# Q rows loaded in natural order from pair 13 on, filler products beside the first scatter, and two GpSimd loads moved behind it

## The chip, the cores and the metric

The kernel runs on one core of one Trainium2 chip. The metric is device time in microseconds (us), the median over runs: 372.13 us over 4 runs, from 369.82 to 373.18. The profile is of one further execution of 369.75 us, whose traced span is 368.1 us.

## The reference

Attention over batch 8, 8 heads, 576 tokens, head size 64, with a window of 32 tokens to each side and 8 global tokens, then a two-matrix block with a squared ReLU.

```python
scores = scale * np.matmul(q, k.transpose(0, 1, 3, 2))
mask = np.abs(pos[:, None] - pos[None, :]) <= window          # window = 32
mask = mask | is_global[:, None] | is_global[None, :]         # 8 global tokens
attn = softmax(np.where(mask, scores, -1e9)); x = np.matmul(attn, v)
h = x @ w_in; r = np.maximum(h, 0.0)                          # 4608x512 @ 512x2048
out = (s * (r * r) + b) @ w_out                               # 2048x512
```

## The kernel before

**Pairs.** Two heads of one batch are a pair; there are 32 (four to a batch), and the kernel walks through them in order. The 576 keys of a head are cut into five chunks of 120 plus the 8 global keys (128 in all). For a pair, `qk` (L479) does per chunk one matmul of K against the queries in its band, an exponential on ScalarE and a mask multiplication on VectorE; `pv` (L498) multiplies the result with V and with ones; `norm_steps` (L516) normalises on ScalarE and VectorE and writes the columns of `xt`, the transposed input of the second block. The global queries' rows are put into `xt` at positions read from the input by `scatter` (L552), eight small copies on GpSimd for a batch.

**The second block** is a generator, `moe_quanta` (L563). Each step is four matmuls of 128x128 by 128x512. `run_pair` (L649) puts about eight such steps between the eight slots of each pair, so that TensorE always has work. It can begin for a batch only after that batch's `scatter`. With the order of work written out by hand, each engine takes its instructions strictly in program order.

**Loads.** A DMA is issued by GpSimd (POOL's queue) or by SyncE (SP's queue). Pairs 0 to 7 are loaded "six rows to a partition": 96 partitions, each with six consecutive tokens of two heads (`load_kq`, L153, GpSimd, rounding to bf16 on the way). From pair 8 (`NSIX`) on, K comes in natural order (one token to a partition, five chunks of 120, `load_nat`, L161, two DMAs) in fp32, is rounded by `round_k` (L182) and transposed by a DMA, `turn_k` (L204). Q still comes six rows to a partition by one DMA (`load_q`, L188), is rounded on ScalarE by `round_q` (L199), and transposed on TensorE by `trans` (L422): six transposes of 96 columns (L430) and one of a zero tile of 4 columns (L436). `trans_b` (L462) copies the transposed Q out of PSUM in two VectorE copies (L469), one a head, and undoes the six-row order in the same copy: the inner step of what it reads is 96 elements. Loads are issued at the start of pair p for pair p + 5 (L886).

**The beginning.** Pairs 0 to 4 run in `first_pair` (L718), with no second block between them; single matmuls of a zero tile whose product nobody reads (`warm`, L712) are put in instead. In pair 1, slot 2, `globals_of`'s last two steps (`move`, L387) turn the global V rows of batch 0 on TensorE and leave their copies to SBUF (`gvx`, L394, ScalarE) on the list `later`, which is emptied in slot 3 behind that slot's exponential and the `rep` activation. `put_v` (L404) then writes them into `vring`, which `pv(0)` reads. GpSimd issues `load_kq(6)` and `load_v(6)` after pair 2, `load_w_out(1)` after pair 3, then does `scatter(0)` (L839), then issues `load_w_out(2)`, `load_kq(7)`, `load_v(7)`, `load_w_out(3)` (L849 to L852) and, at pair 4, `gather(1)` (L892): two indirect DMAs that fetch the global K and Q rows of the next batches into `gf`. Pair 5, slot 7, rounds `gf` to `gb` on VectorE (L366) and pair 6, slot 1, transposes `gb` on TensorE (`turn`, L373).

Of the kernel before, what the change touches and what calls it, by code (L numbers as in the profile page):

```python
# [16 lines left out]
P = 128  # L17
B, H, S, D = 8, 8, 576, 64
NG = 8
# [8 lines left out]
NCH = 5  # L28
KC = 120
HB = 60  # L30
# [5 lines left out]
NR = 5  # L36
NV = 4
NJ = 6
NP6 = S // NJ
NSIX = 8  # L40
KT0 = 16
NX = 3
N6 = NCH * KC // NJ
# [10 lines left out]
def view(ap, *dims):  # L54

    return bass.AP(
        tensor=ap.tensor, offset=ap.offset, ap=[list(ap.ap[0])] + [list(d) for d in dims]
    )
# [8 lines left out]
def kernel(  # L67
# [12 lines left out]
    nc = tc.nc  # L80
# [30 lines left out]
    six = {t: const.tile([P, NR, 2, NJ, D], BF16, name=f"six{t}", tag=f"six{t}") for t in "kq"}  # L111


    natk = const.tile([P, NV, NCH, 2, D], FP32)
    natb = const.tile([P, NV, NCH * P], BF16)

    natq = const.tile([P, NV, 2, NJ, D], FP32)

    xt = const.tile([P, 4, NX * S + 2 * HB * NCH - S], BF16)
    natv = const.tile([P, NV, NCH, 2, D], FP32)  # L120
# [5 lines left out]
    for t, eng in (("k", nc.sync), ("q", nc.scalar)):  # L126
        eng.dma_start(
            out=six0[t].rearrange("p (h x) -> p h x", h=2),
            in_=src[t][0, 0:2].rearrange("h (p j) d -> p h (j d)", j=NJ),
# [5 lines left out]
        out=gidx_p[:],  # L135
        in_=bass.AP(
            tensor=global_idx.tensor, offset=global_idx.offset, ap=[[0, P // NG], [1, NG], [1, 1]]
        ),
# [3 lines left out]
    qbufs = [const.tile([P, 2, LQ], BF16, name=f"qbd{i}", tag=f"qbd{i}") for i in range(3)]  # L142
# [17 lines left out]

    def load_nat(eng, t, p):  # L161
        bi, hp = divmod(p, 4)
        dst = natv if t == "v" else natk
        r = NG if t == "v" else 0
        for hh in range(2):
            o = src[t][bi, 2 * hp + hh, 0, 0].offset

            runs = [(0, NCH, KC)]
            if p == NPAIR - 1 and hh == 1:
                runs = [(0, NCH - 1, KC), (NCH - 1, 1, S - KC * (NCH - 1))]  # L170
            for c, nch, n in runs:
                eng.dma_start(
                    out=dst[r : r + n, p % NV, c : c + nch, hh],
                    in_=bass.AP(
                        tensor=src[t].tensor, offset=o + c * KC * D,
                        ap=[[D, n], [KC * D, nch], [1, D]],
                    ),
                )
# [7 lines left out]
        )  # L186

    def load_q(p):  # L188
        bi, hp = divmod(p, 4)
        nc.sync.dma_start(  # L190
            out=natq[:NP6, p % NV].rearrange("p h j d -> p h (j d)"),
            in_=q[bi, 2 * hp : 2 * hp + 2].rearrange("h (p j) d -> p h (j d)", j=NJ),
        )

    def qrow(p):
        flat = six["q"][:NP6, p % NR].rearrange("p h j d -> p (h j d)")
        return flat.rearrange("p (j h d) -> p j h d", j=NJ, h=2)

    def round_q(p):  # L199
        nc.scalar.copy(  # L200
            out=qrow(p).rearrange("p j h d -> p h j d"), in_=natq[:NP6, p % NV]
        )

    def turn_k(p):  # L204
        kts[p] = kqp.tile([P, KT0 + NCH * P], BF16, tag="kt", name="kt")
        nc.sync.dma_start_transpose(
            out=kts[p][:, KT0:].rearrange("p (c x) -> p c x", x=P), in_=natb[:, p % NV]
        )

    def load_v(eng, p):  # L210
        load_nat(eng, "v", p)
# [13 lines left out]
    dummy = const.tile([P, DM], BF16)  # L225
# [11 lines left out]
    for t in gqd:  # L237
# [18 lines left out]
    ident = const.tile([P, P], BF16)  # L256
# [4 lines left out]
        out=part[:], in0=rowi[:], scalar1=3, scalar2=7,  # L261
# [5 lines left out]
        out=half[:], in0=partf[:], scalar=2.0 * S, in1=half[:], op0=OP.mult, op1=OP.add  # L267
    )
    nc.vector.tensor_copy(
        out=six["k"][:NP6, 0].rearrange("p h j d -> p (h j d)"), in_=six0["k"]  # L270
# [48 lines left out]
    for t in gadd:  # L319
# [7 lines left out]
        out=band[:], in0=band[:], scalar1=(float(WIN) + 0.5) ** 2, scalar2=None, op0=OP.is_le  # L327
# [14 lines left out]
    def load_w_out(j):  # L342
        nc.gpsimd.dma_start(
            out=wout_t[:, 4 * j : 4 * j + 4], in_=w_out2[:, 4 * j : 4 * j + 4]
        )
# [7 lines left out]
    def flush():  # L353
        ops, later[:] = list(later), []
        for f in ops:
            f()
# [65 lines left out]
    def trans(t, p):  # L422
        if p < 6:
            ps = ps_m.tile([P, LQ], BF16, tag="moe", name="pst")
        else:
            ps = ps_s.tile([P, LQ], BF16, tag="s", name="pst")
        for j in range(NJ):
            n = N6 if j == NJ - 1 else NP6
            if t == "q" and p >= NSIX:
                nc.tensor.transpose(  # L430
                    ps[:, NP6 * j : NP6 * j + NP6],
                    qrow(p)[:, j].rearrange("p h d -> p (h d)"), ident[:NP6, :NP6],
                )
                if n > NP6:
                    x = n - NP6
                    nc.tensor.transpose(  # L436
                        ps[:, NP6 * NJ : NP6 * NJ + x], dummy[:x, 0:P], ident[:x, :x]
                    )
                continue
            for hh in range(2):  # L440
                nc.tensor.transpose(  # L441
                    ps[D * hh : D * hh + D, NP6 * j : NP6 * j + n],
                    six[t][:n, p % NR, hh, j], ident[:n, :n],
                )
        return ps
# [16 lines left out]
    def trans_b(p, later=later):  # L462
        ps = trans("q", p)

        def evac():
            n = HB // NJ
            for hh, eng in ((1, nc.scalar.copy if p < 6 else V), (0, V)):
                r = slice(D * hh, D * hh + D)
                eng(  # L469
                    out=view(qbufs[p % 3][r, hh], [P, NCH], [HB + NG, 2], [NJ, n], [1, NJ]),  # L470
                    in_=view(ps[r], [2 * n, NCH], [n, 2], [1, n], [NP6, NJ]),
                )
            if p >= NSIX:
                ktile[p] = kts[p][:, KT0 - NG : KT0 - NG + LQ]
                put_kq(p)

        later.append(evac)
# [74 lines left out]
    def scatter(bi):  # L552

        for i in range(NG):
            nc.gpsimd.tensor_copy(  # L555
                out=xt[:, :, S * (bi % NX) : S * (bi % NX) + S][:, :, ds(greg_p[i], 1)],
                in_=xgs[bi][:, :, i : i + 1],
            )
# [90 lines left out]
    def run_pair(p, nq, extra):  # L649
# [4 lines left out]
        for s in range(8) if p > 4 else range(NCH, 8):  # L654
            prev, later[:] = list(later), []
            now = []
            if s < NCH:
# [3 lines left out]
                if s == 4 and hp == 0 and bi > 1:  # L661
                    later.append(lambda: scatter(bi - 1))
                if s == 2 and NSIX <= p + 2 < NPAIR:
                    cast_v(G, p + 2)
            elif s == 5:
                if p + 1 < NSIX:
                    cast_v(A, p + 1)
                if 4 < p < NPAIR - 1:
                    trans_b(p + 1, now)
            elif s == 6 and 4 < p < NSIX - 1:  # L670
                trans_a(p + 1, now)
            for f in now + prev:
                f()
            if s == 0:
                pv(p - 1)
                pending.extend(norm_steps(p - 1))
            if s == 7 and p + 1 < NSIX:
                put_v(V, p + 1)
# [33 lines left out]
    def warm(n, ps=None):  # L712

        ps = ps or idle_bank()
        for _ in range(n):
            nc.tensor.matmul(ps[:], dummy[:, 0:P], dummy[:])  # L716

    def first_pair(p, extra={}):  # L718
# [40 lines left out]
        out=sel6[:], in0=view(idx6[:], [1, NJ], [0, NG]),  # L759
# [9 lines left out]
    for j in range(2):  # L769
        nc.gpsimd.dma_start(  # L770
            out=win_t[:, :, 1024 * j : 1024 * j + 1024],
            in_=w_in2[:, :, 1024 * j : 1024 * j + 1024],
# [10 lines left out]
        out=vkey[:], in0=kidx[:], scalar1=float(S) - 0.5, scalar2=None, op0=OP.is_le  # L783
    )
    for i in range(2):
        c = i * (NCH - 1)
        nc.vector.tensor_copy(
            out=gadd[i][:, GAP : GAP + NG], in_=view(vkey[:, c : c + 1], [0, NG])
# [3 lines left out]
        out=sel[:], in0=view(kidx[:], [1, NCH], [0, NG]),  # L792
# [8 lines left out]
    steps0 = globals_of(0)  # L801
# [16 lines left out]
    for p in (1, 2, 3, 4):  # L818
        first_pair(p, {
            0: [steps0[1], steps0[2]],  # L820
            2: steps0[3:],
            3: [lambda: put_v(V, 0)],
        } if p == 1 else {})
        if p == 1:
            for j in (1, 2, 3):
                put_v(None, j)
            load_v(nc.gpsimd, 5)
            load_w_out(0)
            greg_p = [
                nc.gpsimd.value_load(g32[:1, i, 0:1], min_val=0, max_val=S - 1)  # L830
                for i in range(NG)
            ]
        elif p == 2:
            load_kq(6)
            load_v(nc.gpsimd, 6)
        elif p == 3:
            load_w_out(1)
    flush()
    scatter(0)  # L839
    for i in (1, 2, 3):  # L840
        rows_of(i)
    gvall = const.tile([NG, (B - 2) * H * D], BF16)
# [2 lines left out]
    nc.sync.dma_start(  # L845
        out=view(natb[96:P], [DM, NV * NCH * P // DM], [1, DM]),
        in_=view(dummy[96:P], [0, NV * NCH * P // DM], [1, DM]),
    )
    load_w_out(2)  # L849
    load_kq(7)  # L850
# [25 lines left out]
    for p in range(4, NPAIR):  # L876
# [16 lines left out]
        if p == 5:  # L893
            for i in range(NG):
                nc.gpsimd.dma_start(
                    out=gvall[i : i + 1].rearrange("o (b h d) -> o b h d", b=B - 2, h=H),
                    in_=v[2:, :, ds(greg_p[i], 1), :].rearrange("b h o d -> o b h d"),
# [6 lines left out]
        if p >= 6 and p + 2 < NPAIR:  # L904
# [4 lines left out]
            for i, j in enumerate(todo):  # L909
                if j < NPAIR:  # L910
                    x = 4 if p in (8, 9) else 4 * i
# [66 lines left out]
```

## Time and profile before

| what | value |
|---|---|
| median of 4 runs | 372.13 us (369.82 to 373.18) |
| profiled execution, its span | 369.75 us, 368.1 us |
| TensorE busy | 349.8 us, 95% of the span |
| VectorE, ScalarE, GpSimd busy | 253.0, 229.9, 82.1 us |
| mean granted TensorE clock | 0.975 |
| Q copies out of PSUM on VectorE (L469) | 58 of 780 ns |
| Q transposes, six-row form, pairs 8 to 31 (L430, L436) | 144 and 24 |
| Q rounding on ScalarE (L200), K rounding (L183) | 24 of 842 ns, 24 of 733 ns |
| DMA share of its 16 engines, 42 to 57 us and 117 to 301 us | 1.21 and 0.57 |

How to read it: TensorE's busy time counts modelled ends of pipelined matmuls, so a busy TensorE is not one at its peak. A row of the timeline gives start, duration, engine, line, operation, output and inputs, the count of merged instructions, and in brackets the idle time ahead of it and what ended it. Rows "POOL ... DMA" are issues, not transfers. The DMA share adds up the time that packets took on 16 engines; since packets overlap on an engine it can pass 1.

### The profile page before, as it was taken

To read this page: it belongs to the slowest core of one execution; us is meant where nothing else is said; L and a number is where in the kernel's file an instruction comes from. 1 tells how busy PE (TensorE), PEld (TensorE's weight loads), DVE (VectorE), ACT (ScalarE), POOL (GpSimd) and SP (SyncE) were. 2 spreads that over 40 slices of the span, in tenths; PEclk is the share of its full clock that TensorE was granted. 3 is DMA by queue.
4 is the path that set the end of the run, shared out by engine and by line. 5 is a ranking of instruction groups with operands and counts; after the bars stand their busy time and mean duration, and the time that the engine had idled before them with its cause. 6 is when DMAs were issued, how large, how long until landed. Compare 5 with 4: busy or idle time off the path is not lost.

```text
span 368.1 us, 7826 instructions
## 1 busy us (share of the span) xinstructions
PE 349.8 (95%) x2824; PEld 184.2 (50%) x2824; DVE 253.0 (69%) x636; ACT 229.9 (62%) x439; POOL 82.1 (22%) x164
## 2 busy tenths in 40 slices
PE   6679799899999999999999999999999999999996
PEld 2344344455545445567655555455557644444444
DVE  6667677867777898878878887788787743423421
ACT  6669589657876677657766776677647742612610
POOL 6964852122032211133103100311020001000000
PEclk9669899999999999999999999999999999999999
DMA  5999999999877777756538973883332011002002
GB/s 123 187 186 215 197 215 195 177 189 251 138 183 175 171 165 177 176 119 122 123 108 232 198 165 108 231 188 82 104 117 68 2 59 57 0 30 86 0 32 85
DMA packets 101440, 50.00 MB, mean 136 GB/s; under 512 B 84224, under 2 KB 94368, under 8 KB 101400
## 3 DMA queue, kind: packets, MB, share of 16 engines
q1 hardware_dynamic: 92360, 37.03, 46.6%
q0 software_dynamic: 8544, 12.03, 16.1%
q8 instruction: 22, 0.36, 0.5%
q10 hardware_dynamic: 496, 0.43, 0.4%
q14 instruction: 18, 0.15, 0.2%
HBM read 41.97 MB, written 9.44 MB: 140 GB/s over the span
## 4 chain that ended last, share of the span: by engine, by line
PE 73%; DVE 8%; DMA 5%; ACT 4%; POOL 4%; issue 3%; SPq 1%; ACTq 0%; POOLq 0%
PE psh L578 29%; PE pso L597 25%; PE po L507 8%; PE pss L481 6%; DVE qbd L469 3%; DMA gf<-in_q_dram,grow 2%; PE pst L430 2%; DMA sixq<-in_q_dram 1%; POOL gf L289 1%; PE psw L716 1%; PE pst L441 1%; ACT ln L538 1%; DMA natq<-in_q_dram 1%; DVE em L488 1%; DMA natv<-in_v_dram 1%
## 5 line engine op out<-in xcount | busy, mean ns | idle before, releaser
L578 PE MATMUL psh<-xt,win_t 128*128 128x512 bf16 (+2 forms) x704 | 140.4, 344 | 2.6 <-POOL xt L555 2.6
L597 PE MATMUL pso<-wout_t,g 128*128 128x512 bf16 (+1 forms) x592 | 137.3, 374 | 0.0
L585 ACT ACTIVATE r<-psh 128x512 bf16<-128x512 f32 x144 | 88.5, 614 | 61.3 <-PE psh L578 55.5
L485 ACT ACTIVATE e<-pss 128x384 bf16<-128x384 f32 (+1 forms) x160 | 76.6, 482 | 50.9 <-PE pss L481 49.9
L578 PEld LDWEIGHTS <-win_t 128*128 128x128 bf16 x704 | 63.6, 98 | 57.8 <-issue 5.1
L588 DVE TENSOR_TENSOR g<-r 128x512 bf16<-128x512 bf16 x144 | 59.6, 428 | 39.9 <-ACT r L585 39.6
L597 PEld LDWEIGHTS <-g 128*128 128x128 bf16 x592 | 55.8, 98 | 59.3
L488 DVE TENSOR_TENSOR em<-e,mask 128x384 bf16<-128x384 bf16 (+1 forms) x160 | 61.8, 389 | 26.9 <-ACT e L485 26.9
L481 PE MATMUL pss<-qbd,kt 128*128 128x384 bf16 (+1 forms) x160 | 52.1, 328 | 5.3 <-DVE qbd L417 2.5
L469 DVE COPY qbd<-pst 64x600 bf16<-64x600 bf16 x58 | 45.2, 780 | 5.5 <-ACT qbd L469 4.3
L555 POOL COPY xt<-xg 128x4 bf16 x64 | 15.3, 239 | 95.9 <-DVE xt L544 92.3
L617 DVE SCALAR_TENSOR_TENSOR osb<-pso,s_bc,bias_row 128x512 f32<-128x512 f32 (+1 forms) x25 | 18.1, 725 | 26.9 <-PE pso L597 26.9
L214 POOL CAST vring<-natv 128x640 bf16<-128x640 f32 x27 | 22.2, 827 | 60.1 <-PE po L507 33.4
L481 PEld LDWEIGHTS <-kt 128*128 128x128 bf16 x160 | 15.7, 99 | 26.0 <-DVE qbd L417 7.0
L544 DVE TENSOR_TENSOR xt<-po,rep 128x600 bf16<-128x600 f32 x32 | 25.0, 780 | 2.4 <-ACT rep L541 1.1
L538 ACT ACTIVATE ln<-po 128x640 f32<-128x640 f32 x32 | 22.5, 703 | 5.7 <-PE po L507 5.4
L541 ACT ACTIVATE rep<-ln 128x640 f32<-128x640 f32 x32 | 24.1, 752 | 0.1
L507 PE MATMUL po<-em,vring 128*64 128x160 bf16 (+3 forms) x448 | 19.7, 224 | 2.3 <-DVE vring L406 1.9
L507 PEld LDWEIGHTS <-vring 128*64 128x64 bf16 x448 | 15.5, 110 | 11.4 <-issue 6.6
L200 ACT CAST sixq<-natq 96x768 bf16<-96x768 f32 x24 | 20.2, 842 | 0.0
L507 PE MATMUL po<-em,onesb 128*64 128x160 bf16 (+2 forms) x448 | 19.7, 226 | 0.2 <-DVE xt L544 0.2
L183 ACT CAST natb<-natk 120x640 bf16<-120x640 f32 x24 | 17.6, 733 | 0.0
(104 smaller groups left out, 211.7 us busy)
## 6 DMA issues: line engine op xcount, KB each, us to landing
natv<-in_v_dram SPq DMA_DIRECT2D x55, 150.0 KB
natk<-in_k_dram SPq DMA_DIRECT2D x47, 150.0 KB
natq<-in_q_dram SPq DMA_DIRECT2D x24, 288.0 KB
out_dram<-osb SPq DMA_DIRECT2D x23, 256.0 KB
wst<-in_moe_w_out_dram POOLq DMA_DIRECT2D x8, 512.0 KB, 5.3
out_dram<-osbh SPq DMA_DIRECT2D x9, 256.0 KB
win_t<-in_moe_w_in_dram POOLq DMA_DIRECT2D x2, 1024.0 KB, 16.0
wout_t<-in_moe_w_out_dram POOLq DMA_DIRECT2D x4, 512.0 KB, 10.5
```

The source lines that it names most:

```text
L469: eng(out=view(qbufs[p % 3][r, hh], [P, NCH], [HB + NG, 2], [NJ, n], [1, NJ]), in_=view(ps[r], [2 * n, NCH], [n, 2], [1, n], [NP6, NJ]),)
L481: nc.tensor.matmul(ps[:], ktile[p][:, P * c : P * c + P], qbufs[p % 3][:, :, LO[c] : HI[c]])
L485: nc.scalar.activation(e[:], ps[:], AF.Exp, scale=SCALE)
L488: later.append(lambda: nc.vector.tensor_mul(em[:], e[:], masks[c]))
L507: nc.tensor.matmul(po[D * hh : D * hh + D, a : a + n], onesb[:] if part else vring[:, p % NV, c, hh], emt[(p, c)][:, hh, x : x + n], start ...
L538: nc.scalar.activation(ln[:], po[:, LQ : 2 * LQ], AF.Ln)
L541: nc.scalar.activation(rep[:], ln[:], AF.Exp, scale=-1.0)
L544: lambda: nc.vector.tensor_tensor(out=view(xt[:, hp, x0:], [KC, NCH], [HB, 2], [1, HB]), in0=halves(po[:, 0:LQ]), in1=halves(rep[:]), op=O ...
L578: nc.tensor.matmul(psh[:, d0 : d0 + n], win_t[:, a, f * P : f * P + P], xt[:, a, x0 : x0 + n], start=(a == 0 and j == 0), stop=(a == 3), s ...
L585: nc.scalar.activation(r[:], psh[:], AF.Relu)
L588: later.append(lambda g=g, r=r: nc.vector.tensor_mul(g[:], r[:], r[:]))
L597: nc.tensor.matmul(pso[:, 0:nn], gl[f][:, u * P : u * P + P], wout_t[:, f, n0 : n0 + nn], start=(f == 0), stop=(f == 15),)
```

## The change

1. From pair 13 (`NSIXQ`) on, `load_q` loads Q in natural order, like K: two DMAs of 120 partitions by five chunks instead of one of 96 partitions (for the last pair one more, for the short chunk). `round_q` copies 120x640 elements straight, `trans` does five transposes of 128 columns over all 128 partitions, and `trans_b`'s two copies read PSUM with inner step 1.
2. For pairs 8 to 12 the sixth transpose takes 100 rows, and the transpose of the zero tile goes. Its rows 96 to 127 are zeroed once by a new DMA on SP.
3. In pair 1, slot 2, `later` is emptied at once (`flush`), so that the two `gvx` copies stand ahead of slot 3's exponential and `rep`.
4. Ahead of `scatter(0)`, 12 matmuls of the zero tile (`warm(12)`) are put on TensorE.
5. `load_w_out(1)` and `load_v(6)` are issued after `scatter(0)` instead of ahead of it.

```diff
+NSIXQ = 13
 def load_nat(eng, t, p):
-        dst = natv if t == "v" else natk
+        if t == "q":
+            dst = natq[:].rearrange("p n h j d -> p n (h j d)")[:, :, 0 : NCH * 2 * D]
+            dst = dst.rearrange("p n (c h d) -> p n c h d", c=NCH, h=2)
+        else:
+            dst = natv if t == "v" else natk
 def load_q(p):
+        if p >= NSIXQ:
+            load_nat(nc.sync, "q", p)
+            return
+    def qnat(p):
+        return six["q"][:, p % NR].rearrange("p h j d -> p (h j d)")[:, 0 : NCH * P]
 def round_q(p):
+        if p >= NSIXQ:
+            nc.scalar.copy(
+                out=qnat(p)[0:KC],
+                in_=natq[0:KC, p % NV].rearrange("p h j d -> p (h j d)")[:, 0 : NCH * P],
+            )
+            return
 def trans(t, p):
+        if p >= NSIXQ:
+            for c in range(NCH):
+                nc.tensor.transpose(
+                    ps[:, P * c : P * c + P], qnat(p)[:, P * c : P * c + P], ident[:]
+                )
+            return ps
             if t == "q" and p >= NSIX:
                 nc.tensor.transpose(
-                    ps[:, NP6 * j : NP6 * j + NP6],
-                    qrow(p)[:, j].rearrange("p h d -> p (h d)"), ident[:NP6, :NP6],
+                    ps[:, NP6 * j : NP6 * j + n],
+                    qrow(p)[:n, j].rearrange("p h d -> p (h d)"), ident[:n, :n],
                 )
-                if n > NP6:
-                    x = n - NP6
-                    nc.tensor.transpose(
-                        ps[:, NP6 * NJ : NP6 * NJ + x], dummy[:x, 0:P], ident[:x, :x]
-                    )
 def trans_b(p):
+                if p >= NSIXQ:
+                    eng(
+                        out=view(qbufs[p % 3][r, hh], [P, NCH], [HB + NG, 2], [1, HB]),
+                        in_=view(ps[r], [P, NCH], [HB, 2], [1, HB]),
+                    )
+                    continue
 for p in (1, 2, 3, 4):
-            2: steps0[3:],
+            2: [*steps0[3:], flush],
         elif p == 2:
             load_kq(6)
-            load_v(nc.gpsimd, 6)
-        elif p == 3:
-            load_w_out(1)
     flush()
+    warm(12)
     scatter(0)
+    load_w_out(1)
+    load_v(nc.gpsimd, 6)
...
+    nc.sync.dma_start(
+        out=view(six["q"][96:P], [384, 10], [1, 384]), in_=view(dummy[96:P], [0, 10], [1, 384])
+    )
     load_w_out(2)
```

More of the change, by code (lines that the diff above doesn't have):

```diff
@@ L195, in qrow @@
     def qrow(p):
-        flat = six["q"][:NP6, p % NR].rearrange("p h j d -> p (h j d)")
+        flat = six["q"][:, p % NR].rearrange("p h j d -> p (h j d)")
         return flat.rearrange("p (j h d) -> p j h d", j=NJ, h=2)
+    def qnat(p):
+        return six["q"][:, p % NR].rearrange("p h j d -> p (h j d)")[:, 0 : NCH * P]
     def round_q(p):
+        if p >= NSIXQ:
[4 more added lines that the diff above has]
+            return
         nc.scalar.copy(
-            out=qrow(p).rearrange("p j h d -> p h j d"), in_=natq[:NP6, p % NV]
+            out=qrow(p)[:NP6].rearrange("p j h d -> p h j d"), in_=natq[:NP6, p % NV]
         )
```

## The prediction

> **What bounds the kernel now.** I read the page's busy line first (TensorE 349.8 us of 368.1), then the chain that ended last, then the timeline of each stage that the change touches. From 66 us on TensorE is the bound: in the window 117 to 301 us it is busy 182.38 of 184 us, so there every TensorE nanosecond saved counts, and the only waits are short ones at pair boundaries, on VectorE's Q copies. Before 66 us it is loads and waits. The chain, in order of time, around the first scatter:
>
> ```profile
> 41.57 0.77 POOL wout_t L343
> 44.55 0.92 POOL natv L172
> 46.56 1.04 POOL gf L289
> 47.91 8.71 DMA gf<-in_q_dram,grow
> 57.52 0.73 ACT natb L183
> ```
>
> The start of pair 6 hangs on the gather of global rows, which GpSimd issues at 47.91 us and which lands 8.7 us later. The timelines (start, duration, engine, line, operation; in brackets the idle time before) of TensorE, then VectorE:
>
> ```profile
> 41.58 4.44 PE L578 MATMUL psh<-xt,win_t 128*128 128x512 bf16 x12 [2.64 <-POOL xt L555]
> 45.85 0.30 PE L481 MATMUL pss<-qbd,kt 128*128 128x320 bf16 x1
> ...
> 56.92 0.25 PE L373 MATMUL psg<-ident,gb 64*64 64x64 bf16 x4 [0.41 <-DVE gb L366]
> ...
> 65.92 0.31 PE L481 MATMUL pss<-qbd,kt 128*128 128x320 bf16 x1 [1.17 <-DVE qbd L417]
> ```
>
> ```profile
> 56.64 0.23 DVE L366 CAST gb<-gf 128x128 bf16<-128x128 f32 x1 [0.68 <-DMA gf<-in_q_dram,grow]
> ```
>
> So the 2.64 us wait for the scatter is real, but TensorE waits for `gf` 15 us later even so: a gain before 56.5 us is kept only if `gf` comes sooner. GpSimd's queue:
>
> ```profile
> 37.56 0.80 POOL L343 DMA_DIRECT2D wout_t<-in_moe_w_out_dram  x1
> 38.96 2.57 POOL L555 COPY xt<-xg 128x4 bf16 x8 [0.61 <-DVE xt L544]
> 41.57 0.77 POOL L343 DMA_DIRECT2D wout_t<-in_moe_w_out_dram  x1
> 42.33 0.68 POOL L156 DMA_DIRECT2D sixk<-in_k_dram  x1
> 42.99 0.65 POOL L156 DMA_DIRECT2D sixq<-in_q_dram  x1
> 43.63 1.84 POOL L172 DMA_DIRECT2D natv<-in_v_dram  x2
> 45.45 0.81 POOL L343 DMA_DIRECT2D wout_t<-in_moe_w_out_dram  x1
> 46.56 1.04 POOL L289 DMA_INDIRECT gf<-in_k_dram,grow  x1 [0.30 <-issue]
> 47.91 0.98 POOL L289 DMA_INDIRECT gf<-in_q_dram,grow  x1 [0.30 <-issue]
> ```
>
> The scatter is not held up by the two issues ahead of it: GpSimd is free at 38.36 and then waits 0.61 us for VectorE. And the DMA engines are full (share 1.21 from 42 to 57 us), landing GpSimd's loads in order of issue: by the DMA view, `load_kq(6)`'s Q lands at 34.71 + 7.6 = 42.3, `load_w_out(1)` at 37.56 + 8.2 = 45.8, `gf` at 56.6. The gather is late because of the bytes ahead of it.
>
> [...] after the 2.64 us idle the clock is 0.60 from 41.6 to 45.9, and after 1.90 us at 22 to 24 us it is 0.54 from 25.0 to 28.6. [...] L469 (step 96) takes 775 ns for 600 elements, while the step-1 copies of 64 elements (L377) take 184. [...]
>
> **The change, part by part.** All against the profiled 369.75 us (span 368.1 and 1.65 around it), 2.38 below the median; I carry differences over to the median.
>
> *Natural Q, TensorE.* Around 108.7 us the six transposes and the zero tile last from 108.70 to 109.16, 0.46 us. The starts of the six take about 0.26, so the zero tile costs 0.20. Five of 128 columns: [...] scaling the traced 43 ns for 96 columns gives 57. Pairs 13 to 31: 19 x (0.46 - 0.28) = -3.4. Pairs 8 to 12: 5 x 0.20 = -1.0. TensorE is full, so -4.4 counts in full; ends -2 [...] and -4.8.
>
> *Natural Q, VectorE.* [...] Two copies a pair, 19 pairs: -11.9 us of VectorE, which is not the bound. What it buys are boundary waits on L469 and L417: 0.36 at 121.6, 0.60 at 160, and 0.11, 0.09, 0.13, 0.13, 0.19, together -1.6. If the copies stay at 775: 0.
>
> *Natural Q, ScalarE, SP, DMA.* 19 x (842 - 733) = -2.1 us of ScalarE, hidden behind TensorE. SP issues one more DMA a pair, about 0.5 us on a queue that issues 4.4 us in a 9.4 us pair; queued behind are `load_v`, `turn_k` and `put_v`, needed two pairs later. A load becomes 1200 packets of 256 bytes instead of 192 of 1536: at 23 against 90 ns mean, 27.6 against 17.3 us over 16 engines, +0.6 us a pair, share +0.07 upon 0.57. Loads have some 20 us in hand. Cost 0; if the share reached 1 each pair would pay the 0.6.
>
> *Flush.* The gvx copies start at about 20.8 instead of 22.68, `put_v` at 21.5 instead of 23.27, `pv(0)` up to 1.8 us sooner; the exponential behind them starts 0.2 later. But `pv(1)` needs the `vring` DMA, issued at 23.32 and only 0.9 earlier at best (GpSimd's cast ends 22.4), and pair 5's Q lands at 21.07 + 15.9 = 36.97, 0.7 before its use at 37.66. I take -0.5 at 38.95 (0 to -0.7).
>
> *warm(12).* 12 x 0.216 = 2.6 us fills the 2.64 wait, at no cost. It keeps the clock: the 12 products behind take 2.6 instead of 4.27, -1.7. TensorE is ready for `turn` at 56.51 - 0.5 - 1.7 = 54.3.
>
> *The two issues, and the SP fill.* `load_w_out(1)` and `load_v(6)` go behind the scatter, with `load_w_out(2)`, `load_kq(7)`, `load_v(7)`, `load_w_out(3)` and the gather queued after them: 0.80 + 1.83 us of issue, less 0.5. More important, GpSimd's DMA queue runs dry when `load_kq(6)` lands at 42.3, while the next load, issued at 41.0, moves its first bytes about 2 us later (a `gf` on idle engines lands 2.5 us after its issue). Lost: a gap of 0.8, the head start that the two loads had (0.3), the 240 KB fill of rows 96 to 127 (1.2 us at 200 GB/s, 0.8 of it in the gap, so 0.4), and SP's loads of pair 8 starting 2.2 us sooner with a third of the engines (0.7): +2.2, so `gf` lands near 58.8. Bounds: 0 (the queue stays full) and +4.5 (SP takes half). `turn` then starts at 59.1: TensorE idles 4.8 us instead of 0.41. So the -2.2 gained is all spent and +2.2 is added. [...] +1.6 (0 to 1.8). The 1.17 us wait at 65.92, where VectorE is behind, shrinks by about 0.6. Sum of the beginning: +2.2 + 1.6 - 0.6 = +3.2.
>
> *Total.* -4.4 - 1.6 + 3.2 = -2.8: 366.95 in the profile, 369.3 as a median.
>
> **The rivals.** *The gather is not late* (0.34): the queue's backlog hides the later issue, `gf` lands at 56.6 as before. For it: the shares stay over 1 up to 57 us, and `gf` is bounded by bytes, not by its issue. Against: 0.8 MB of those bytes lie behind the scatter now. TensorE then idles 2.6 us before `turn`, half a chance of 1.6 us of slow clock: -6.0 + 0.8 = -5.2, 366.9.
> *The gather is much later* (0.13), the one on the slower side: the re-queued loads fall behind SP's loads of pairs 8 to 10, so each goes at half rate. In the 4 us from 52.7 to 56.6 the last `load_w_out` needed 3.3 us beside SP, against 2.1 alone; with six loads at that pace `gf` lands near 64. It decides from +6 us in all, a landing at 61.4 with the clock's cost. At 64: +7.4 + 1.6 - 0.6 - 6.0 = +2.4, 374.5.
> *The copies don't speed up* (0.06): [...] -2.8 + 1.6 = -1.2, 370.9.
>
> **How the numbers follow.** The likeliest (0.47) is the sum, 369.3, its own range 367.3 to 371.3. The range to hold 8 in 10 goes from 365.3 (the gather on time and a little of the clock's cost saved) to 373.8 (a gather some 4 us later than that). A measurement of this kernel can tell about 1% (3.7 us) from no change. Faster by over 1% (under 368.4): 0.30 from the first rival, 0.11 from the main case's lower end, 0.41. Slower by over 1% (over 375.9): the far end of the second, 0.09. Within: 0.50.
>
> **What would show it.** L469 in natural form near 460 ns and about 12 us less VectorE work; five transposes in 0.28 us; no zero-tile transposes; the 12 `psh` products at about 41 us in 2.6 us; `gf`'s Q landing near 59, a wait of 4 to 5 us at L373 and a clock well under 1 after it. Wrong would be: a `gf` landing by 57 (then the first rival), data waits on natural Q after 100 us, or boundary waits that stay although the copies are shorter.

## The result, and the profile after

The changed kernel takes 369.65 us (median of 32 runs, 368.06 to 370.79) beside 370.94 us of the kernel before in the same comparison (median of 53 runs, 369.02 to 373.9): ratio 0.9958, 95% interval 0.9944 to 0.9971, so 1.1 to 2.1 us faster, 1.56 by the ratio. That is within 1%, on the side and in the range forecast; the forecast of -2.8 lies outside the interval. The two profiled executions do not show the gain: 369.69 us (span 368.0) against 369.75 (span 368.1). They are one execution each, so the stages are compared instead, each from the first `pss` product of one pair to that of a later one. The table has the experiments too, which are explained below; us:

| kernel | pairs 0 to 7 end at | 7 to 13 | 13 to 31 | 31 to the end | span |
|---|---|---|---|---|---|
| before | 65.92 | 55.70 | 170.66 | 75.82 | 368.10 |
| **after** | **73.06** | **54.66** | **164.80** | **75.52** | **368.04** |
| e1, the issues put back | 68.86 | 55.28 | 164.80 | 75.51 | 364.45 |
| e3, natural Q only | 67.61 | 55.23 | 164.80 | 75.51 | 363.15 |
| e4, the move only | 73.51 | 56.30 | 170.69 | 75.82 | 376.32 |
| e5, `warm` only | 68.52 | 55.70 | 170.64 | 75.83 | 370.69 |
| e6, no zero tile, six-row Q | 67.60 | 55.86 | 168.59 | 75.75 | 367.80 |
| e9, flush only | 66.41 | 56.29 | 170.68 | 75.82 | 369.20 |

The column "13 to 31" answers one question exactly: it is 170.64 to 170.69 with six-row Q and its zero tile, and 164.80 with natural Q, in every kernel of the table. In the changed kernel the stages from pair 7 to the end, called the middle below, give 7.2 us (1.04 + 5.86 + 0.30), and the beginning takes 7.1 of it away in this execution. The first two columns are less steady. With the old Q, "7 to 13" lies between 55.70 and 56.30. Two of the experiments, e7 and e11, have the code of the changed kernel up to pair 13; their pairs 0 to 7 end at 73.69 and 71.66 us, where this profile has 73.06.

VectorE's Q copies, in the page's costliest groups (count, then busy us and mean ns, then the idle time before them), first before, then after in both forms:

```profile
L469 DVE COPY qbd<-pst 64x600 bf16<-64x600 bf16 x58 | 45.2, 780 | 5.5 <-ACT qbd L469 4.3
```

```profile
L494 DVE COPY qbd<-pst 64x600 bf16<-64x600 bf16 x20 | 15.6, 778 | 4.8 <-ACT qbd L494 4.5
L489 DVE COPY qbd<-pst 64x600 bf16<-64x600 bf16 x38 | 17.8, 468 | 0.9
```

The same 600 elements take 778 ns in the six-row form and 468 in the natural one; the forecast said near 460. That figure was an estimate of mine which the profile of before did not show. VectorE's busy time falls from 253.0 to 240.2 us.

TensorE's timeline around the first scatter, and on to the turn of pair 6:

```profile
40.08 2.76 PE L741 MATMUL psw<-dummy 128*128 128x512 bf16 x12
42.78 2.75 PE L603 MATMUL psh<-xt,win_t 128*128 128x512 bf16 x12
45.37 0.30 PE L506 MATMUL pss<-qbd,kt 128*128 128x320 bf16 x1
...
63.12 0.32 PE L391 MATMUL psg<-ident,gb 64*64 64x64 bf16 x4 [7.06 <-DVE gb L384]
63.37 1.89 PE L603 MATMUL psh<-xt,win_t 128*128 128x512 bf16 x4
```

Before, the line behind the turn reads:

```profile
57.10 1.04 PE L578 MATMUL psh<-xt,win_t 128*128 128x512 bf16 x4
```

The unread products fill the wait for the scatter, and the 12 `psh` products behind them take 2.59 us from first start to the next product (45.37 - 42.78) where they took 4.27. Then the gain is handed over: the wait at the turn, 0.41 us before, is 7.06, and four products after it take 1.89 us instead of 1.04, on half the clock (0.50 from 63 to 67 us). The chain that ended last goes through the same place:

```profile
50.40 1.01 POOL gf L307
51.72 11.10 DMA gf<-in_q_dram,grow
```

The gather is issued at 51.72 instead of 47.91 us and lands 11.1 us later instead of 8.7. GpSimd's timeline says what came ahead of it:

```profile
34.45 0.64 POOL L158 DMA_DIRECT2D sixq<-in_q_dram  x1
40.17 2.56 POOL L580 COPY xt<-xg 128x4 bf16 x8 [5.08 <-DVE xt L569]
42.77 0.76 POOL L361 DMA_DIRECT2D wout_t<-in_moe_w_out_dram  x1
43.52 1.83 POOL L178 DMA_DIRECT2D natv<-in_v_dram  x2
```

GpSimd sits idle for 5.08 us ahead of the scatter, and between 34.45 and 42.77 us it issues no load. What that does to the DMA engines stands in the windows (busy us and instructions of TensorE, its weight loads, VectorE, ScalarE, GpSimd; then clock, DMA share, GB/s), first before, then after:

```profile
40.00:44.50 4.50, 2.92 (x9) 1.12 (x9) 2.62 (x12) 1.25 (x4) 4.22 (x9) 0.76 1.15 191
```

```profile
40.00:44.50 4.50, 4.50 (x28) 1.98 (x23) 3.03 (x13) 2.40 (x5) 3.87 (x11) 1.00 0.34 67
63.00:67.00 4.00, 3.88 (x13) 1.49 (x14) 2.34 (x11) 1.60 (x3) 1.90 (x4) 0.50 1.11 216
```

In 40 to 44.5 us TensorE goes from 2.92 busy at a clock of 0.76 to full, which is what the `warm` line is for, and the DMA engines go from 191 to 67 GB/s. (191 - 67) x 4.5 us = 0.56 MB were not moved in that stretch: 2.8 us of transfer at 200 GB/s, the rate of before from 42 to 57 us. The line from 63 us on has the slow clock that follows the wait, 0.50.

### The profile page after: what moved, and what is told of

Read it like the earlier page. It is cut to its first block, busy times and chain, and to the rows that moved or that the text cites. A ratio compares the mean times of both kernels' runs of the same rounds, so it can differ in the third digit from the quotient of the medians.

```text
span 368.0 us, 7804 instructions
## 1 busy us (share of the span) xinstructions
PE 348.6 (95%) x2793; PEld 184.4 (50%) x2793; DVE 240.2 (65%) x636; ACT 227.9 (62%) x439; POOL 85.4 (23%) x164
## 4 chain that ended last, share of the span: by engine, by line
PE 78%; DVE 6%; DMA 5%; POOL 4%; issue 3%; ACT 2%; POOLq 0%; ACTq 0%
PE pso L622 31%; PE psh L603 30%; PE po L532 8%; PE pss L506 6%; DMA gf<-in_q_dram,grow 3%; DVE qbd L494 2%; PE pst L447 2%; PE pst L460 1%; DMA sixq<-in_q_dram 1%; POOL gf L307 1%; DMA natk<-in_k_dram 1%; POOL natv L178 1%; DVE em L513 1%; PE psw L741 1%; DVE kt L431 1%
## 5 line engine op out<-in xcount | busy, mean ns | idle before, releaser
L513 DVE TENSOR_TENSOR em<-e,mask 128x384 bf16<-128x384 bf16 (+1 forms) x160 | 59.4, 374 | 29.5 <-ACT e L510 29.4
L580 POOL COPY xt<-xg 128x4 bf16 x64 | 19.2, 299 | 99.2 <-DVE xt L569 95.8
L494 DVE COPY qbd<-pst 64x600 bf16<-64x600 bf16 x20 | 15.6, 778 | 4.8 <-ACT qbd L494 4.5
L489 DVE COPY qbd<-pst 64x600 bf16<-64x600 bf16 x38 | 17.8, 468 | 0.9
```

Of the source, the lines that this page charges most:

```text
L494: eng(out=view(qbufs[p % 3][r, hh], [P, NCH], [HB + NG, 2], [NJ, n], [1, NJ]), in_=view(ps[r], [2 * n, NCH], [n, 2], [1, n], [NP6, NJ]),)
L513: later.append(lambda: nc.vector.tensor_mul(em[:], e[:], masks[c]))
```

## The experiments

The theory when they began: the middle's gain is the form of Q; the beginning's loss is the move of the two issues, which empties GpSimd's DMA queue and makes `gf` late. The rivals: the loss comes from SP's side (its earlier loads and the 240 KB fill) or from the flush; the middle's gain is TensorE's alone.

**e1: the two issues back, everything else as changed.**

```
         load_kq(6)
+        load_v(nc.gpsimd, 6)
+    elif p == 3:
+        load_w_out(1)
...
     scatter(0)
-    load_w_out(1)
-    load_v(nc.gpsimd, 6)
```

> The changed kernel with load_v(6) and load_w_out(1) issued ahead of the scatter again. Theory (the two loads behind the scatter leave GpSimd's DMA queue dry for some 4 us and put 0.8 MB ahead of the gather): gf's Q lands by 58 instead of 62.8, the wait at the transposes of gb falls from 7.1 us to about 3, and the kernel is 5 to 7 us faster than before, near 364.5. Rival (the lateness comes from the fill of the spare Q rows on SP, or from the scatter itself being 1.2 us late after the flush): gf still lands at 61 or later and the time stays within 1.5 us of the changed kernel.

Measured: 366.03 us, ratio 0.9823 (0.9772 to 0.9874). So in the changed kernel the move costs about 5 us by the runs (3.6 between the two profiled spans). `gf` lands at 59.12 instead of 62.82, later than the 58 expected. TensorE at the turn:

```profile
59.43 0.25 PE L391 MATMUL psg<-ident,gb 64*64 64x64 bf16 x4 [3.57 <-DVE gb L384]
```

Half of the wait goes with the move. The scatter's copies start at 39.99 us, after GpSimd has waited 0.88 us for VectorE, and at 40.17 us with the issues behind it: the two issues ahead of the scatter had not held it up.

**e3: natural Q only**, on the kernel before (with the fill of rows 96 to 127 that it needs).

> The kernel before with the Q parts alone (natural rows from pair 13, no zero tile for pairs 8 to 12, the fill on SP); no flush, no filler products, issues where they were. Theory (the whole gain of the middle, 7.2 us from pair 7 to the end, comes from the form of Q): 6 to 7.5 us faster than before. Rival (part of those 7.2 us is the engines catching up after the long wait at pair 6, so that it is not there without that wait): 3 to 5 us faster.

Measured: 365.18 us, 0.9819 (0.9782 to 0.9856). That is 6.7 us by the ratio, as the theory had it (5.0 between the profiled spans), and the stages from pair 7 on give 6.6 (0.47 + 5.86 + 0.31). The changed kernel has 0.6 more there, all of it in pairs 7 to 13; the rival of catching up would explain that part, but no run shows that it does. The waits list of TensorE from 117 to 301 us has no wait for VectorE left; before has three there, 1.2 us in all. `gf` lands at 57.44, only 0.8 later than before, and TensorE does not wait for it, so the fill is cheap for the gather where the queue stays full. Pair 7 starts 1.7 us later than before all the same: ScalarE stands for 2.46 us ahead of an exponential at 49.71 us (2.38 us in e6, in no other kernel), and the profile names nothing that it waited for.

**e4: the move only**, the e1 diff reversed, on the kernel before.

> The kernel before with the two issues moved behind the scatter, nothing else. Theory: the queue runs dry from about 42 to 43.6, gf lands at 59 to 61, TensorE waits 3 to 4.5 us at the transposes of gb and the clock halves after it: 3 to 6 us slower than before. Rival (the move costs nothing by itself, the lateness needs the flush or the fill): within 1 us of before.

Measured: 376.48 us, 1.0112 (1.0073 to 1.0152). `gf` is issued at 52.27 and lands at 63.26, the turn waits 5.31 us, and the DMA rate in 40 to 44.5 us is 25 GB/s. With no other edit the move makes the kernel 4.2 us slower, within the 3 to 6 expected; the landing and the wait are both longer than expected.

**e5: `warm(12)` only**, on the kernel before.

```
     flush()
+    warm(12)
     scatter(0)
```

> The kernel before with the 12 filler products ahead of the scatter alone. Theory (the 1.7 us of clock that they save are spent at the wait for gf, which is bounded by the DMA queue): the 12 products behind the scatter take 2.7 us instead of 4.4, the wait at the transposes of gb grows from 0.4 to 2 us or more, and the time is within 1.5 us of before. Rival (the gain is kept): 1.7 us faster or more.

Measured: 372.23 us, 1.0031 (1.0008 to 1.0054). TensorE's timeline of it:

```profile
42.37 2.75 PE L578 MATMUL psh<-xt,win_t 128*128 128x512 bf16 x12
...
59.08 0.25 PE L373 MATMUL psg<-ident,gb 64*64 64x64 bf16 x4 [3.47 <-DVE gb L366]
```

The products are fast and the time gained is waited away at the turn, as the forecast said of a gain ahead of `gf`; here `gf` also landed 2.2 us later (58.78 against 56.62), which was not forecast, and the clock was half from 59.9 to 63.3 (the four products behind the turn took 1.28 us instead of 1.04). The edit by itself gains nothing and costs a little.

**e9: the flush only**, on the kernel before.

```
-            2: steps0[3:],
+            2: [*steps0[3:], flush],
```

> The kernel before with the flush in pair 1 alone. Theory (the flush loses, because VectorE's small copy of gkt into kt then meets GpSimd's DMA issue and its three casts and takes 2.5 us instead of 0.16): that copy takes over 2 us again, pair 2 starts about 1 us later than before, and the end is 0 to 1 us later, since the wait for gf takes up what the beginning gains or loses. Rival (the 2.5 us were chance in one execution): the copy takes about 0.16 us, pair 2 starts 1.5 us sooner, the end is within 0.5 us of before.

Measured: 372.57 us, 0.9999 (0.9984 to 1.0013): nothing. VectorE's and then GpSimd's timeline of it:

```profile
21.11 2.55 DVE L413 COPY kt<-gkt 128x40 bf16<-128x40 bf16 x1
```

```profile
21.57 2.06 POOL L214 CAST vring<-natv 128x640 bf16<-128x640 f32 x3
```

The same copy before:

```profile
20.99 0.17 DVE L413 COPY kt<-gkt 128x40 bf16<-128x40 bf16 x1
```

The `gvx` copies do start sooner, but `put_v(0)` stands on VectorE behind a copy of 40 elements a partition, which lasts 2.55 us and ends within 0.04 us of GpSimd's third cast. The same copy takes 2.55 us in the changed kernel, 2.57 in e1, 2.27 in e3 and 2.02 in e4. Of these profiles it takes 0.17 only in that of before, where it started in a pause of GpSimd's (0.57 us long). The copy's recorded start (21.11) is 0.46 us ahead of the first cast's, more than the 0.17 us that it takes in before, and it lasts until all three casts are done (21.57 + 2.06 = 23.63), not one. The reading is that the casts hold the copy; by what means is not shown.

**e13: those casts moved to ScalarE**, on the changed kernel, to test that reading.

```
-    for p in (1, 2, 3):
-        cast_v(G, p)
...
             for j in (1, 2, 3):
+                cast_v(A, j)
+            for j in (1, 2, 3):
                 put_v(None, j)
```

> The changed kernel with the casts of V for pairs 1 to 3 on ScalarE behind pair 1 instead of on GpSimd ahead of it. Theory (the flush gains nothing because VectorE's small copies, and put_v behind them, wait until GpSimd's casts are done): the copy of gkt ends 2 us sooner, pv(0) starts near 22.2 instead of 24.3, the scatter starts 0.5 to 1.5 us sooner and the end comes 0.5 to 2 us sooner than in the changed kernel. Rival (something else holds those copies): they still take over 2 us.

Measured: 371.25 us, 1.0003 (0.9986 to 1.0021), so about 0.4% slower than the changed kernel. VectorE, then TensorE:

```profile
21.34 0.22 DVE L431 COPY kt<-gkt 128x40 bf16<-128x40 bf16 x1
21.77 0.47 DVE L424 COPY vring<-gvx 8x640 bf16<-8x640 bf16 x1
```

```profile
22.29 1.01 PE L532 MATMUL po<-em,vring 128*64 128x160 bf16 x14
...
30.10 0.61 PE L532 MATMUL po<-em,vring 128*64 128x160 bf16 x14 [2.81 <-DMA vring<-gvx]
```

The hold is gone (0.22 us, though this copy too starts while GpSimd issues a load) and `pv(0)` starts at 22.29 instead of 24.35: the casts were the cause. The next pair's product then waits 2.81 us for the `vring` DMA, and the scatter starts at 41.42 us instead of 40.17, so the forecast of a gain at the end was wrong. Part of that wait is this edit's own: pair 1's cast now comes later, and SyncE issues the DMA at 24.17 us instead of 22.23. Whether the DMA would have held up the flush's gain by itself is not shown.

**e10: the gather first**, on the changed kernel: `gather(1)` ahead of the moved issues.

```
     scatter(0)
-    load_w_out(1)
-    load_v(nc.gpsimd, 6)
     for i in (1, 2, 3):
         rows_of(i)
+    gather(1)
+    load_w_out(1)
+    load_v(nc.gpsimd, 6)
...
-        if p % 8 == 4 and p + 4 < NPAIR:
+        if p % 8 == 4 and 4 < p and p + 4 < NPAIR:
```

> The changed kernel with one thing moved: the gather of the next batches' global rows is issued straight after the scatter, ahead of load_w_out(1), load_v(6) and the rest. Theory (the two moved loads cost time only because the gather is queued behind them): gf lands near 46 to 48, the wait of 7 us at the transposes of gb goes, the clock stays full, and the kernel is 6 to 8 us faster than the changed kernel, 362 to 364. Rival (a queue run dry costs more than the gather: the V and Q rows of pairs 6 and 7 come late as well): waits at the transposes of Q or at V's casts in pairs 5 to 7 take the gather's place, and the kernel stays within 3 us of the changed one.

Measured: 367.99 us, 0.9865 (0.9823 to 0.9907). `gf` lands at 48.05, and the turn still comes late. ScalarE, then TensorE:

```profile
57.08 0.72 ACT L232 CAST vring<-natv 128x640 bf16<-128x640 f32 x1 [5.12 <-DMA natv<-in_v_dram]
```

```profile
59.82 0.25 PE L391 MATMUL psg<-ident,gb 64*64 64x64 bf16 x4 [3.58 <-DVE gb L384]
```

ScalarE stands before the V of pair 6 instead, now behind the gather, with its next activations behind it. The bracket names `gb`, but `gf` had landed 11 us before: the cast of `gb`, at 59.56 us, stood on VectorE behind products that waited 3.70 us for ScalarE. Both forecasts missed: the wait moved, as the rival said, but the kernel is some 3.4 us faster than the changed one, neither 6 to 8 nor under 3. Of the some 5 us that the move costs, the new order thus saves 3.4; the bytes that the empty queue did not move are still missing, now to the V of pair 6.

**e8: natural Q and `warm`, no flush, issues back, gather first.**

> Natural Q and the 12 filler products, no flush, the two loads ahead of the scatter as in the kernel before, and the gather straight after the scatter. Theory: as e10, with no dry queue either; no wait for gf, the 1.7 us of clock kept: 8 to 10 us faster than before, 361 to 364. Rival (the saturated DMA engines deliver whatever is now queued behind the gather late instead): 6 to 7 us faster, no better than natural Q alone.

Measured: 364.81 us, 0.98 (0.9763 to 0.9837): the turn does not wait and the clock is full from 30.6 us on (the four products behind the turn take 1.04 us). That is 7.4 us faster than before, less than the 8 to 10 expected. It is about 1.6% below the changed kernel, the lowest ratio found, but not to be told from e1, e3 or e12. Much of what it saves in the beginning against e3 (pair 7 starts at 65.23 us, not 67.61) it gives back: pairs 7 to 13 take 56.82 us where e3 takes 55.23, in waits of 0.4 to 0.7 us for VectorE at the pair boundaries.

**e12: e8 with natural Q from pair 8** (`NSIXQ = 8`).

> The kernel of e8 (no flush, loads ahead of the scatter, gather straight after it, filler products) with natural Q from pair 8 on instead of 13. Theory (TensorE and the boundary waits bound the pairs from 8 on too): the waits of 0.3 to 0.7 us at 82 to 113 us go and the transposes shrink, 2 to 3.5 us faster than e8, near 361. Rival (the loads for pairs 8 to 12 are issued while the DMA engines are full, and natural rows take 27.6 us of engine time against 17.3): Q comes late, ScalarE waits for it, and it is no faster than e8 or slower.

Measured: 364.6 us, 0.9818 (0.9787 to 0.9848), no better than e8: TensorE waits 1.38 us at 63.9, ahead of pair 7, and pairs 7 to 13 take 58.05 us, with a wait of 2.20 at 82.6. VectorE's line there:

```profile
84.49 0.17 DVE L431 COPY kt<-gkt 128x40 bf16<-128x40 bf16 x1 [3.37 <-DMA kt<-natb]
```

The rival had the time right, but not the wait: it is for K, not for Q. SyncE issues this transposing of K by DMA at 80.59 us, where e8 has it at 77.22. In SyncE's order it stands behind the Q loads, which now need two issues each instead of one; what share of the delay they make is not shown.

**e6: six-row Q throughout, without the zero tile.** The rows 96 to 127 are filled, and the sixth transpose reads 100 rows. The edit is against e3's kernel.

```
-NSIXQ = 13
+NSIXQ = 99
```

> The kernel before with six-row Q to the end, but no zero tile for pairs 8 to 31 (the sixth transpose takes 100 rows, with the fill on SP). Theory (the zero tile costs 0.20 us of a full TensorE in each pair): 24 x 0.20 = 4.8 us faster, between 4 and 5.5. Rival (at pair boundaries TensorE waits for VectorE's Q copies, so that what is saved comes back as a longer wait there): 2 to 3.5 us faster.

Measured: 369.59 us, 0.9912 (0.988 to 0.9943), 3.3 us faster, as the rival had it. The stage from 13 to 31 is what it was made for. TensorE has 18 x 0.196 = 3.5 us less to do and the stage is 2.07 shorter. The waits of TensorE from 117 to 301 us (total, times, longest), before and then in e6:

```profile
PE pss L481 <- DVE qbd L417: 1.2, 3, 0.6
```

```profile
PE pss L506 <- DVE qbd L435: 3.2, 8, 0.8
```

So what TensorE saved came back as waits for VectorE. In pairs 7 to 13, where five zero tiles went, nothing was gained (55.86 against 55.70). Natural Q's transposes are no shorter than these (0.279 us against 0.262), yet with it the stage is another 3.79 shorter, and the 3.2 us of waits are gone. What differs is VectorE's Q copy, 0.31 us each of two, and ScalarE's rounding (752 ns in the changed kernel against 842).

**e7 and e11: the natural copy made longer,** to isolate it: in e7 it walks the elements in another order, in e11 it is a product with ones.

```
-                        out=view(qbufs[p % 3][r, hh], [P, NCH], [HB + NG, 2], [1, HB]),
-                        in_=view(ps[r], [P, NCH], [HB, 2], [1, HB]),
+                        out=view(qbufs[p % 3][r, hh], [P, NCH], [1, HB], [HB + NG, 2]),
+                        in_=view(ps[r], [P, NCH], [1, HB], [HB, 2]),
```

```
-                    eng(
+                    nc.vector.tensor_tensor(
...
+                        in1=view(onesb[r], [0, NCH], [0, 2], [1, HB]), op=OP.mult,
```

> The changed kernel with the natural Q copied out of PSUM in another order of the same elements, so that the inner step is not 1. Theory (step 1 is what makes the copies short, and the shorter copies end the waits at the pair boundaries): the copies take about 775 ns again, VectorE works 12 us more, the boundary waits come back, and the kernel is 1.5 to 2.5 us slower than the changed one. Rival (the copies are off the path): the copies take 775 ns and the time is within 0.7 us of the changed kernel.

> The changed kernel with the natural Q taken out of PSUM by a multiplication with ones of the same elements in the same order, in place of the copy; the transposes stay natural. Theory (the short copies end the boundary waits, which are the part of the middle's 7.2 us that the transposes don't explain): each takes 700 to 800 ns instead of 468, boundary waits of 0.1 to 0.8 us stand at most pairs from 13 on, and the kernel is 1.5 to 3 us slower than the changed one. Rival (TensorE's shorter transposes are nearly all of it): within 0.7 us of the changed kernel.

Measured: e7 480.04 us, 1.2867 (1.2843 to 1.2891); e11 369.5 us, 0.9963 (0.9947 to 0.9979). Groups of VectorE, e7 and then e11:

```profile
L489 DVE COPY qbd<-pst 64x600 bf16<-64x600 bf16 x38 | 107.1, 2820 | 1.3 <-PE pst L447 0.3
```

```profile
L489 DVE TENSOR_TENSOR qbd<-pst,onesb 64x600 bf16<-64x600 bf16 x38 | 17.8, 468 | 0.9
```

Neither reached the 775 ns that it was made for. At 2820 ns the copies are plainly on the path (waits of 3.2 to 4.5 us a pair), and at 468 nothing changes; neither says what 775 would cost. e6 beside e3 is the nearest to it.

## Why the prediction was right, and where it was not

**The time and the order of the reasons held.** The forecast was a gain in the middle, mostly spent by a late `gf`, total -2.8; measured -1.56. The median of 369.65 us lies closer to the 369.3 forecast than that, but only since the kernel before came out at 370.94 and not at the 372.13 of its first four runs. The parts add up within their intervals, which together leave some 0.006 open: e3 -0.0181, e4 +0.0112, e5 +0.0031, e9 -0.0001 give -0.0039, the change -0.0042. With the middle's -7.2, the runs' -1.56 leaves +5.6 for the beginning, between the profile's +7.1 and the forecast's +3.2. So two terms were too small, by 1.2 us in the middle and 2.4 in the beginning, with opposite signs; that they partly cancel is luck.

**TensorE, -4.4: right in the durations, not in what they are worth.** From the first transpose to the next product of the other block it is 0.458 us before, 0.279 with five natural transposes and 0.262 with six and no zero tile: 19 x 0.179 = 3.40 and 5 x 0.196 = 0.98, as worked out. But "TensorE is full, so -4.4 counts in full" is a step that e6 contradicts: 3.5 us taken from TensorE alone gave 2.07, since the pair boundaries then waited longer for VectorE.

**Boundary waits, -1.6: too small.** The middle gave 7.2 where the two terms make 6.0. I had called VectorE "not the bound" from its busy share, and counted only the idle times that the trace shows. By e6 and e3, 3.8 of the 5.86 us between pairs 13 and 31 need the shorter copies (or ScalarE's, which was not tried apart). Part of the difference may be how a wait is recorded: in the traces a product's modelled end comes 379 ns after its start while the next one can start after 216, so a traced wait of 0.3 us may be 0.46. The seven waits that I had listed would make 1.1 us more; that is a reckoning, not shown.

**`warm`, -1.7 of clock and a covered wait: right** to 0.1 us (2.59 against 4.27), and spent at the turn, as e5 shows alone.

**The flush, -0.5: wrong.** The step that failed is `put_v` at 21.5 us: it came at 23.83, and at 23.93 in e9, behind the held copy, and e13 shows that GpSimd's casts held it. The working rested on a 0.17 us copy of one profile, which the other profiles do not repeat. The time of e9 could not show a gain here, since one made ahead of the turn is waited away at it; the scatter shows 0.2 at most, at 39.57 us in e9 against 38.96, with pair 0 starting 0.79 us later. A note on that start: pair 0 begins at 8.92 us in before, e3 and e6 and at 9.55 to 9.71 in after, e4, e8 and e9. No edit goes with it, and e11, the changed kernel's code up to pair 13, has 8.92, so 0.6 of the +7.1 is no part of the change.

**The queue gap, +0.8, and `gf` at 58.8: the mechanism right, the size too small.** This is the term that was mis-sized most. I put the scatter's end at 41.0; it came at 42.73, 1.2 us later than before's where I had it 0.5 sooner. And `load_kq(6)` landed at 41.06 instead of 42.3: its last packet ends at 40.7, and the next load's first one starts at 44.2. So the queue was dry for 3.5 us, not 0.8, and it was thin before that: from 40 to 44.5 us it moved 0.05 MB, where the kernel before moved 0.86. SP took what was free: from 36 us to the landing of `gf` it moved 1.40 MB instead of 0.81. Both together, 0.56 MB not moved and 0.59 MB moved for others, are some 5.7 us at 200 GB/s, near the 6.2 by which `gf` is late (62.82 against 56.62; 61.42 and 63.79 in e11 and e7). e4, with neither flush nor `warm` nor natural Q, lands it at 63.26, so the move is the cause. The same sum for e4 gives 5.4 us (0.75 MB not moved, 0.33 MB more for SP) of 6.6. e1 puts the rest of the change at +2.5.

**The clock after the wait, +1.6: a little small.** The term was an estimate of mine. The clock is half from 60.4 to 67.2 us (0.50), twice as long as in before after the 2.64 us wait (0.50 from 42.4 to 45.7 us) and after the 3.5 us waits of e1 and e5 (3.4 us each), and 4.1 us of it lie after the turn; at half speed that loses about 2 by estimate, just over the upper end given (1.8).

**The rivals.** "The gather is not late" fell. "Much later", put at 64, was nearer to where `gf` landed (62.8) than the likeliest case, and its point of decision, 61.4, was passed; it did not end slower because the middle gave 1.2 more than the forecast, and because the landing is 1.2 short of 64. "The copies don't speed up" fell at once (468 ns).

**Open.** How much of the middle's gain is VectorE's copy and how much ScalarE's shorter one. Why e5's `gf` is 2.2 us late with no load moved: it is issued 0.8 us later (48.7 against 47.9), SP moves 0.2 MB more until then (1 us at 200 GB/s), and whether these are the reason is not shown. What ScalarE waits for in e3 and e6. How GpSimd's casts hold a copy that starts ahead of them.

## What to carry to other kernels

Before moving DMA issues behind a compute step on the same engine, ask what is still in flight at the end of that step: a queue that ran dry for 3.5 us was paid for by a consumer further down the queue, here 15 us later, and what filler products gained in between was waited away there. Where two engines meet at every pair boundary, a saving on the busier one may not count in full unless the other gets shorter too (here 3.5 us saved gave 2.07, and with the shorter copies 5.86). A stage that repeats to 0.05 us between kernels, like pairs 13 to 31 here, says more of an edit than the medians of whole runs.

## What the hardware showed unexpectedly

- A bf16 product of a PSUM tile with an SBUF tile took the 468 ns of the plain copy of the same 600 elements (38 of each, e11 and after), where I had expected 700 to 800 ns.
- The same copy with the element order changed took 2820 ns (e7), six times as long. It reads with an inner step of 60 and writes with one of 68, in runs of two elements; the six-row form, which reads with a step of 96 in runs of six and writes with step 1, takes 778. Which of these differences costs the time is not shown.
- A copy of 40 elements a partition on VectorE took 0.17 us in a pause of GpSimd's and 0.22 us beside its issue of a load, but 2.02 to 2.57 us where GpSimd's casts followed without such a pause (after, e1, e3, e4 and e9).
